# A long convolution by two-stage transforms and a gated token mixer: the first transform group gets a work list of its own

## The chip, the cores and the metric

The kernel runs on one core of a Trainium2 chip. TensorE (PE) multiplies matrices into PSUM; VectorE (DVE) and ScalarE (ACT) empty PSUM and do the elementwise work; GpSimd (POOL) makes index tables and starts some of the transfers, SyncE (SP) most of the others. The metric is the device time of one execution in microseconds (us). Three runs of the kernel before took 2020.13, 2022.82 and 2023.51 us, median 2022.82.

## The reference, cut to what matters

`x` is (8, 5696, 128), `h` is (5696, 128). The first half is a causal convolution along the sequence, per channel, by Fourier transforms; the second mixes its result over the tokens and the channels.

```
Xf, Hf = rfft(x, 2S), rfft(h, 2S)                # S = 5696
x = irfft(Xf * Hf)[:, :S]                        # the convolution
theta = x @ w_theta
y = w_tok_r @ (x*cos(theta)) + w_tok_i @ (x*sin(theta))    # over the 5696 tokens
u = x + y
out = u + relu(u @ w_ch)
```

## The kernel before, in words

**Groups.** The convolution is done in eight groups: two batch entries and half of the channels each (`groups`, dh outer). A group has four stages, each cut into chunks; every chunk fills one of four PSUM buffers (`psum()`, pool of four) and one engine empties it.

- **a** (`stage_a`, L255): 16 chunks of 4 matmuls, a short transform of 89 rows. Its input `x16` has one buffer, loaded by 16 POOL transfers (`load_x`, L139), which can start when the `a` of the group before has read it. The result is emptied by ACT (L262) or by DVE (L260).
- **f** (`spectrum`, L278): 12 chunks of up to 32 matmuls, the second transform, emptied by ACT into a buffer `xs` (L394) of the pool `fs`, which has three.
- **p, q** (`products`, L398): on DVE, per chunk of f one product for each of the two batch entries, of `xs` with the spectrum of `h`, into `uv[0]` and `uv[1]`. The last one of a chunk frees its `xs`.
- **c** (`stage_c`, L419): 16 chunks of 16 matmuls, the way back, emptied by ACT (L425) or DVE (L423) into `g`. Chunks 0 to 7 read `uv[0]`, 8 to 15 read `uv[1]`.
- **d** (`stage_d`, L443): 7 chunks with the twiddle table `e_t` as an operand, emptied by ACT (L449) or DVE (L447) into `yt`, which is stored at the end of the group.

**Work lists.** DVE and ACT run in the order in which the program issues their work (`tc.manual_schedule`). For a group the order is written as a string, `PLAN`, that `run_plan` walks through: a lower-case letter is a chunk emptied by ACT, a capital one emptied by DVE. In the list of group g the letters c and d are group g's, the letters a, f, p and q those of group g+1. `r` is a q that was left over from the group before, for the last chunks (`LATE` of them, three).

**The first group.** It does not go by the list. After `a` of group 0 (`a0`), twelve steps `b_step` (one f, then both its products) run with the two small tables `r_u`, `r_v` woven in (`r_table`, an index part on POOL, then DVE and ACT). Then `woven` merges c of group 0, a of group 1 and the rest of the twiddle tables (`e_left`): `E_STEPS` are seven pieces of five rows, for each of which POOL makes indices (`e_index`, L157, L377, L161), DVE folds them (L164, L167) and ACT takes two sines (L170, L173). The pieces use three areas in the not yet used `yt` buffer and one of their own, `e_more`. After that the letters f, p, q, d, D of `PLAN` run.

**After the groups.** The last group runs with the first 15 phase steps (`phase_step`, in the order of `tile_order`) woven into its c and d. Their input `ya0` is loaded by POOL, its last tile of 128 tokens by SP into a small area (`load_ya0_end`). From about 400 us on the token mixing runs, a long row of matmuls at L1305 that the weights of the ring (L640) feed.

```
PLAN = "aaaAcrAaCaccrArcAacAcAacAcaAcCfCfcpfpCpccqqqfffqpqdfppqffdqpdqpDffpdqfpdpDp"
```

Of the kernel before, what the change touches and what calls it, by code (L numbers as in the profile page):

```python
# [10 lines left out]
F32 = mybir.dt.float32  # L11
BF16 = mybir.dt.bfloat16
# [11 lines left out]
def kernel(  # L24
# [82 lines left out]
    def pool(name, bufs, stack, **kw):  # L107
        return stack.enter_context(tc.tile_pool(name=name, bufs=bufs, **kw))
# [4 lines left out]
    NE, WB, BT = 9, 6 * 4 * CJ * 64, 7 * 1024  # L113
    keep = pool("keep", 1, ctx, side="right")
    fc = pool("fft_c", 1, conv, side="right")
    fs = pool("fft_s", 3, conv, side="right")
    fy = pool("fft_y", 1, conv, side="right")
    s1 = pool("set_1", 1, setup, side="right")

# [43 lines left out]
    def below_one(t, k):  # L163
        nc.vector.scalar_tensor_tensor(t, k, MAGIC, t, op0=ALU.subtract, op1=ALU.subtract)  # L164
# [181 lines left out]
    r_v = fc.tile([P, P], F16)  # L346
    e_t = fc.tile([P, EN, 2, NB], F16)

    def r_table(n_, r_):
        t, k = (s1.tile([P, 2 * N2], F32, name=f"r_{n_}{q}") for q in "tk")  # L350
        index(k, [[0, 2], [1, N2]], 0)
        nc.gpsimd.tensor_scalar(t, k, lane[:, 0:1], 1.0 / N2, op0=mult, op1=mult)
        for q0 in range(2):
            for q1 in range(2):
                a_ = t[64 * q0:64 * q0 + 64, 64 * q1:64 * q1 + 64]
                nc.gpsimd.tensor_scalar(a_, a_, 0.25 * (1 + (1 - n_ if q0 else n_) + q0 - q1), None, op0=add)
        up(t, k, nc.gpsimd)
        below_one(t, k)
        sine(k, t, 1)
        r2, k2 = (z.rearrange("p (r n) -> p r n", r=2) for z in (r_, k))  # L360
        nc.scalar.activation(r2[:, :, :EN], k2[:, :, :EN], AF.Copy, scale=0.125)
        nc.scalar.activation(r2[:, :, EN:], k2[:, :, EN:], AF.Copy, scale=-0.125)

    ES = 5
    e_all = fy.tile([P, NB, N2], BF16, tag="yt", name="e_all").rearrange("p m n -> p (m n)").bitcast(F32)
    first = ExitStack()
    e_more = pool("set_e", 1, first).tile([P, 2 * ES * NB], F32, name="e_more")
    E_STEPS = [(n, n0, min(ES, EN - n0)) for n, n0 in enumerate(range(0, EN, ES))]

    def e_pair(n, cn):  # L370
        at = e_more if n % 4 == 3 else e_all[:, 2 * (n % 4) * ES * NB:]
        return [at[:N1, q * ES * NB:][:, :cn * NB] for q in range(2)]

    def e_index(n, n0, cn):
# [95 lines left out]
    a_chunk, (spectrum, products) = front(0)  # L470
    a0 = steps_of(a_chunk, NA, (2, 4, 6, 8, 10, 12, 14))

    def b_step(c):
        spectrum(c)
        for e in range(2):
            products(c, e)

    b0 = [lambda c=c: b_step(c) for c in range(NCK)]
    BATCH = ((0, 4), (4, 4), (8, 3), (11, 1))
    for c in range(NCK):  # L480
        h_chunk(c)
# [4 lines left out]
        h_store(c0, n)  # L486
    for e_ in E_STEPS[:4]:
        e_index(*e_)
    for t, dst, mul in ((w_in[0], w_theta_sb, 1.0 / (2.0 * math.pi)), (w_in[1], w_ch_sb, 1.0)):
        nc.gpsimd.tensor_scalar(dst, t, mul, None, op0=mult)  # L490
    for n, f in enumerate(a0):
# [138 lines left out]
    def yt_room():  # L630
        return small(0, 4 * P).rearrange("p (b n) -> p b n", b=4)
# [17 lines left out]
    def open_phases():  # L649
# [6 lines left out]
        nc.gpsimd.tensor_scalar(w_neg, w_theta_sb, -1.0, None, op0=mult)  # L656
        st["turns"] = (ones, plus, minus, w_neg)

    def load_ya0():
        sides["phases"]["ya0"] = only = ExitStack()  # L660
        ya = sides["phases"][0] = pool("s2a", 1, only, reuse_waits="tile").tile([P, 4, H - P], BF16, name="ya0")
        for p_ in range(4):
            to = min((p_ + 1) * QR, H - P)
            nc.gpsimd.dma_start(ya[:, :, p_ * QR:to], yt_hbm[:, 0:4, p_ * QR:to])

    def load_ya0_end():
        ya = sides["phases"]["end"] = yt_room()
        nc.sync.dma_start(ya, yt_hbm[:, 0:4, H - P:H])

    def load_ya1(yt=None):  # L670

# [54 lines left out]
    def phase_step(ti, hh, store=nc.sync, odd_eng=None):  # L726

        st = sides["phases"]
        yT = st["end"] if (hh, ti) == (0, 2 * NJ - 1) else st[hh][:, :, ti * P:(ti + 1) * P]
# [24 lines left out]
    steps0 = [lambda ti=ti, n=n: phase_step(ti, 0, nc.gpsimd if 12 <= n < 15 else nc.sync)  # L754
              for n, ti in enumerate(tile_order)]

# [5 lines left out]
                pump()  # L762
        return both

    PLAN = "aaaAcrAaCaccrArcAacAcAacAcaAcCfCfcpfpCpccqqqfffqpqdfppqffdqpdqpDffpdqfpdpDp"
    LATE = PLAN.count("r")
    assert [sum(PLAN.count(x) for x in z) for z in ("aA", "cC", "f", "p", "qr", "dD")] == [NA, NC, NCK, NCK, NCK, ND]

    def ready_for_phases():
        xin.close()  # L770
# [1 line left out]
        load_ya0()  # L772

    def run_plan(plan, g, a_chunk, c_chunk, d_chunk, spectrum, products, late_products):
        at = {"a": 0, "c": 0, "d": 0, "f": 0, "p": 0, "q": 0, "r": NCK - LATE}
# [18 lines left out]
    late_products = None  # L794
# [573 lines left out]
```

## Time and profile before

| | us |
|---|---|
| three runs, median | 2022.82 (2020.13 to 2023.51) |
| the profiled execution | 2024.96 |
| its span | 2023.2 |
| first matmul of f, group 0 | 44.58 |
| first matmul of c, group 0 | 65.40 |
| first matmul of f, group 1 | 88.2 |
| first ACT eviction of a, group 2 | 109.23 |
| first matmul of f, groups 2 to 7 | 125.8, 159.8, 195.9, 233.1, 266.9, 300.8 |
| last d of the last group | 365.0 |

All times are from the start of the span. A row of a timeline gives the start, the time taken, engine, line, operation, output and inputs, and in square brackets how long the engine had been idle and for whom it waited. A row of the windows view gives for a stretch of time its length, the busy time of each engine with its instructions in brackets, then the granted TensorE clock (1.00 is full speed), the share of the DMA engines and GB/s.

### The profile page before, as it was taken

How to read it: one execution, taken by the hardware profiler on the slowest of the kernel's cores; microseconds unless marked ns; L12 is line 12 of the kernel's file. 1: busy time of each engine (PE TensorE's matmuls, PEld its weight loads, DVE VectorE, ACT ScalarE, POOL GpSimd, SP SyncE). 2: the span in 40 equal slices, each digit the busy share in tenths (PEclk: the TensorE clock that was granted, in tenths of full speed). 3: DMA queues.
4: the chain of work that ended last, by engine and by line, in shares of the span. 5: the costliest groups of instructions: out<-in, count | busy, mean ns of one | idle time of the engine just before them, and what ended most of it. 6: DMA issues, size and time to landing. Idle time of an engine off the chain costs nothing.

```text
span 2023.2 us, 41078 instructions
## 1 busy us (share of the span) xinstructions
PE 1929.2 (95%) x15581; PEld 1073.0 (53%) x15757; DVE 1565.0 (77%) x2900; ACT 646.2 (32%) x954; POOL 963.8 (48%) x1721
## 2 busy tenths in 40 slices
PE   5799998889999999999999999999999999999998
PEld 5799897544444444444444444444444444444444
DVE  8877778776788888888877668777677776877767
ACT  6788998742232323232300000011111111111111
POOL 8523323363454545354656554544535445354550
PEclk9789999899999999999999999999999999999999
DMA  9979878997898989899999799887878878788793
GB/s 113 68 85 136 78 103 206 270 257 143 142 184 171 180 170 167 174 174 180 169 172 154 131 243 230 134 149 128 152 130 148 147 129 150 132 150 143 137 156 84
DMA packets 488230, 312.02 MB, mean 154 GB/s; under 512 B 183415, under 2 KB 449143, under 8 KB 487047
## 3 DMA queue, kind: packets, MB, share of 16 engines
q0 software_dynamic: 321552, 155.16, 61.1%
q1 hardware_dynamic: 159312, 140.47, 23.7%
q10 hardware_dynamic: 7168, 13.76, 1.9%
q8 instruction: 123, 2.02, 0.4%
q14 instruction: 75, 0.61, 0.1%
HBM read 354.37 MB, written 90.29 MB: 220 GB/s over the span
## 4 chain that ended last, share of the span: by engine, by line
PE 64%; DVE 4%; DMA 2%; issue 2%; POOL 1%; ACT 0%; DVEq 0%; SPq 0%; POOLq 0%
PE m L1305 59%; DVE c L1312 2%; PE v L985 1%; PE utp L978 1%; POOL ring L640 1%; PE m L1309 1%; DVE wt L898 1%; PE m L1193 1%; DMA b<-z_hbm 1%; DMA ring<-in_moe_w_tok_r_dram 0%; PE theta_ps L524 0%; PE tpz L926 0%; DMA yT<-yt_hbm 0%; DMA c<-cp_hbm 0%; DMA cp_hbm<-c 0%
## 5 line engine op out<-in xcount | busy, mean ns | idle before, releaser
L640 POOL DMA_DIRECT2D ring<-in_moe_w_tok_i_dram x720 | 388.4, 548 | 661.5 <-DVE wt L898 556.5
L898 DVE STREAM_TRANSPOSE wt<-ring 128x384 f32<-128x384 f32 (+2 forms) x720 | 359.0, 522 | 117.2 <-PE m L1305 63.6
L640 POOL DMA_DIRECT2D ring<-in_moe_w_tok_r_dram x720 | 387.2, 549 | 118.7 <-DVE wt L898 66.4
L1305 PE MATMUL m<-b,wt 128*128 128x512 bf16 x1605 | 384.8, 379 | 4.1 <-DVE wt L898 2.1
L1305 PEld LDWEIGHTS <-wt 128*128 128x128 bf16 x1804 | 176.0, 98 | 216.3 <-DVE wt L898 5.1
L1312 DVE TENSOR_TENSOR c<-c,m 128x512 f32<-128x512 f32 x412 | 265.1, 668 | 0.4 <-PE m L1305 0.4
L980 ACT ACTIVATE ring<-utp 128x512 bf16<-128x512 bf16 x85 | 50.8, 597 | 576.3 <-PE utp L978 576.3
L139 POOL DMA_DIRECT2D x<-in_x_dram x128 | 99.4, 792 | 133.7 <-PE ps L255 126.3
L419 PE MATMUL ps<-r_u,uv 128*128 128x128 f16 x1024 | 126.8, 221 | 4.1 <-DVE g__1336 L423 1.2
L419 PE MATMUL ps<-r_v,uv 128*128 128x128 f16 x1024 | 126.3, 221 | 0.0
L1226 PE MATMUL m<-b,wt 128*128 128x512 bf16 x471 | 113.0, 387 | 12.7 <-DMA b<-zr_hbm 7.8
L398 DVE TENSOR_TENSOR uv<-xs,hs 128x1024 f16<-128x1024 f16 (+1 forms) x192 | 116.7, 661 | 10.4 <-ACT xs L394 9.3
L419 PEld LDWEIGHTS <-uv 128*128 128x128 f16 x2048 | 121.3, 99 | 6.0 <-issue 3.9
L975 ACT ACTIVATE ub<-c 128x512 bf16<-128x512 f32 x88 | 55.1, 628 | 185.9 <-DMA ring<-in_moe_w_tok_i_dram 104.0
L394 ACT ACTIVATE xs<-ps 128x1024 f16<-128x1024 f32 x96 | 88.7, 978 | 13.8 <-PE ps L278 8.8
L1226 PEld LDWEIGHTS <-wt 128*128 128x128 bf16 x528 | 51.4, 99 | 70.2 <-issue 16.3
L928 ACT ACTIVATE ring<-tpz 128x512 bf16<-128x512 bf16 (+1 forms) x46 | 27.5, 597 | 146.3 <-PE tpz L926 126.8
L526 ACT ACTIVATE red<-theta_ps,magic 128x512 f32<-128x512 f32 (+1 forms) x46 | 31.6, 687 | 129.4 <-PE theta_ps L524 98.2
L278 PEld LDWEIGHTS <-w_t 64*128 64x128 f16 x3240 | 60.6, 102 | 21.9 <-issue 15.9
L255 PE MATMUL ps<-f_t,x 89*128 89x180 f16 x512 | 56.0, 251 | 7.7 <-DMA x<-in_x_dram 4.8
L987 DVE SCALAR_TENSOR_TENSOR c<-v,c 128x512 f32<-128x512 f32 x88 | 59.8, 682 | 2.6 <-PE v L985 2.6
L831 DVE TENSOR_TENSOR b<-b 128x1024 bf16<-128x1024 bf16 x100 | 61.3, 679 | 0.0
(2928 smaller groups left out, 3632.0 us busy)
## 6 DMA issues: line engine op xcount, KB each, us to landing
ring<-in_moe_w_tok_r_dram POOLq DMA_DIRECT2D x352, 96.0 KB, 4.7
ring<-in_moe_w_tok_i_dram POOLq DMA_DIRECT2D x352, 96.0 KB, 4.9
ring<-in_moe_w_tok_r_dram POOLq DMA_DIRECT2D x352, 80.0 KB, 4.6
ring<-in_moe_w_tok_i_dram POOLq DMA_DIRECT2D x352, 80.0 KB, 3.9
cp_hbm<-c SPq DMA_DIRECT2D x88, 256.0 KB, 2.3
c<-cp_hbm SPq DMA_DIRECT2D x88, 256.0 KB, 4.6
out_dram<-c SPq DMA_DIRECT2D x88, 256.0 KB, 4.6
yy<-y_hbm SPq DMA_DIRECT2D x84, 128.0 KB, 2.5
```

What stands on the lines that cost most here:

```text
L139: nc.gpsimd.dma_start(x16[p0:p1, e, n0:n0 + 16, :HD], bass.AP(tensor=src.tensor, offset=src.offset + (p0 * N2 + n0) * D + dh * HD, ap=[[N2 ...
L278: nc.tensor.matmul(ps[:, e, j * HD:(j + 1) * HD], w_t2[rows, slot(e, c0 + j), N2 * (1 - ri):N2 * (3 - ri)], a_st["a"][rows, ri * K1 + c0 + ...
L394: nc.scalar.activation(xs[:, :, :, :CHK[c][1]], ps, AF.Copy)
L398: nc.vector.tensor_tensor(uv[e][:, :, :, c0:c0 + ck], xs_of[c][:, e:e + 1, :, :ck].to_broadcast([P, 2, HD, ck]), h_part(c), op=mult)
L419: nc.tensor.matmul(o, uv_t[e][:, r, d * K1:d * K1 + P], r_, start=(r == 0), stop=(r == 1))
L640: nc.gpsimd.dma_start(wb[32 * i:32 * i + 32, :ng, :nj * 64], bass.AP(tensor=a.tensor, offset=a.offset + row0 * S + p * H + i * QR + j0 * 6 ...
L831: return [lambda f=f, x=x: f(*x) for f, x in ((nc.vector.tensor_sub, (bt[M3], b12, b22)), (nc.vector.tensor_sub, (bt[M4], b21, b11)), (nc. ...
L898: nc.vector.transpose(wt.rearrange("p j t r -> p (j t r)").bitcast(F32).rearrange("p (j g t) -> p g j t", j=TJ, g=4)[:, :ng, :nj], wb[:, : ...
L987: nc.vector.scalar_tensor_tensor(c[:m], v[:m], 0.0, c[:m], op0=ALU.max, op1=ALU.add)
L1226: nc.tensor.matmul(ms[n // 2 * 2 + h], a[n][:, j, :, r], bts_of[p][jj][n % 2 * 2 + h][:, r, :], start=(n % 2 == 0 and jj == 0 and r == 0), ...
L1305: nc.tensor.matmul(ms[q], a[q][:, j, :, r], bts[jj][q][:, r, :], start=(jj == 0 and r == 0), stop=(jj == NJ - 1 and r == 1 and q not in left))
L1312: nc.vector.tensor_tensor(c, z, ms[q], op=op)
```

## The change

- The first group goes by lists. `PLAN_X` holds f, p, q of group 0 and `u`, the two small tables; it leaves four q over. `PLAN_0` is the list of group 0 with c, d of group 0, a, f, p, q of group 1, those four q as `r`, and `t`, a piece of the twiddle table: its `e_table` and then the `e_index` of the piece four further on.
- `fs` has four buffers instead of three, and four products are late instead of three.
- `PLAN`, the list of the later groups, is another: of 16 a, 10 are emptied by ACT instead of 8; of 7 d, 4 instead of 5; the first four f, instead of three, stand before the last c.
- The index part of both small tables (`r_index`) is issued with the first indices of the twiddles, and their first DVE step (`below_one`) stands in front of the list. In the built program POOL makes the four first index sets, then those of the small tables one after the other; DVE has the two folding steps behind the tenth and the twelfth of the twelve evictions at L333, so before its first eviction of `a0`.
- The twiddle pieces have four rows (`ES`): nine pieces in four areas of the `yt` buffer; `e_more` goes.
- For room, `ya0` holds 19 tiles instead of 21. Tiles 19 and 20 are loaded by SP into an `xs` buffer when the late products of the last group are issued (`load_ya0_ends`), and their phase steps are the 13th and 14th.

```diff
-    fs = pool("fft_s", 3, conv, side="right")
+    fs = pool("fft_s", 4, conv, side="right")
...
-    def r_table(n_, r_):
-        t, k = (s1.tile([P, 2 * N2], F32, name=f"r_{n_}{q}") for q in "tk")
+    r_at = {}
+
+    def r_index(n_):
+        t, k = r_at[n_] = [s1.tile([P, 2 * N2], F32, name=f"r_{n_}{q}") for q in "tk"]
...
         up(t, k, nc.gpsimd)
-        below_one(t, k)
+
+    def r_table(n_, r_):
+        t, k = r_at[n_]
         sine(k, t, 1)
...
-    ES = 5
+    ES = 4
...
-        at = e_more if n % 4 == 3 else e_all[:, 2 * (n % 4) * ES * NB:]
+        at = e_all[:, 2 * (n % 4) * ES * NB:]
...
     for e_ in E_STEPS[:4]:
         e_index(*e_)
+    for n in range(2):
+        r_index(n)
...
-    woven(b0, ([lambda: r_table(0, r_u), lambda: r_table(1, r_v)], 0.0, 0.6))
-    e_left = [lambda f=f, n=n: f(*E_STEPS[n]) for f, n in (
-        (e_table, 1), (e_index, 5), (e_table, 2), (e_index, 6), (e_table, 3),
-        (e_table, 4), (e_table, 5), (e_table, 6))]
+    for n in range(2):
+        below_one(*r_at[n])
+    PLAN_X = "fqfpqpfffupfqppfqfqpqppqfqffpfuppp"
+    PLAN_0 = "cttCCrcaCaAraraarAaAaacaattAACcftCCpffcfttpCPccccctpqfqfqpfqfpDqddfqpqqfpdpfDpddfppp"
+    PLAN = "aaAarcAarcAaCaacrAarcAacAacCfpfcCccffpCppcccqfqfqfqqpDfqddppfpqdpqfDpffdpDp"
+    LATE = PLAN.count("r")
+    at_ = {"f": 0, "p": 0, "q": 0, "u": 0}
+    for k in PLAN_X:
+        n, at_[k] = at_[k], at_[k] + 1
+        if k == "f":
+            spectrum(n)
+        elif k == "u":
+            r_table(n, (r_u, r_v)[n])
+        else:
+            products(n, "pq".index(k))
...
+    Y_ENDS = 19
...
+    def load_ya0_ends():
+        two = fs.tile([P, 2, HD, CK], F16, tag="xs", name="ya_end").rearrange("p e d k -> p (e d k)").bitcast(BF16)
+        ends_ = sides["phases"]["end"]
+        for q, ti in enumerate(range(Y_ENDS, 2 * NJ - 1)):
+            ends_[ti] = two[:, 4 * P * q:4 * P * (q + 1)].rearrange("p (b n) -> p b n", b=4)
+            nc.sync.dma_start(ends_[ti], yt_hbm[:, 0:4, ti * P:(ti + 1) * P])
...
+    tile_order[12:] = [19, 20] + [ti for ti in tile_order[12:] if ti not in (19, 20)]
...
+            elif k == "t":
+                e_table(*E_STEPS[n])
+                if n + 4 < len(E_STEPS):
+                    e_index(*E_STEPS[n + 4])
...
             for c in range(NCK - LATE, NCK):
                 late_products(c, 1)
+            load_ya0_ends()
...
-        plan = PLAN
-        if g == 0:
-            woven((steps_of(c_chunk, NC, [n for n in range(NC) if n % 2 or n < 8]), 0.06, 1.0),
-                  (steps_of(a_chunk, NA, (5, 11)) + [lambda: load_x(2)], 0.0, 0.55), (e_left, 0.0, 0.9))
-            first.close()
-            plan = [x for x in PLAN if x in "fpqdD"]
-        run_plan(plan, g, a_chunk, c_chunk, d_chunk, spectrum, products, late_products)
+        run_plan(PLAN if g else PLAN_0, g, a_chunk, c_chunk, d_chunk, spectrum, products, late_products)
```

More of the change, by code (lines that the diff above doesn't have):

```diff
@@ L471 @@
     a0 = steps_of(a_chunk, NA, (2, 4, 6, 8, 10, 12, 14))
[L473 to L478, printed above, removed]
     BATCH = ((0, 4), (4, 4), (8, 3), (11, 1))
@@ L498 @@
     in_order.enter_context(tc.manual_schedule(engines={mybir.EngineType.DVE, mybir.EngineType.Activation}))
-    woven(b0, ([lambda: r_table(0, r_u), lambda: r_table(1, r_v)], 0.0, 0.6))
-    e_left = [lambda f=f, n=n: f(*E_STEPS[n]) for f, n in (
-        (e_table, 1), (e_index, 5), (e_table, 2), (e_index, 6), (e_table, 3),
-        (e_table, 4), (e_table, 5), (e_table, 6))]
+    for n in range(2):
+        below_one(*r_at[n])
+    PLAN_X = "fqfpqpfffupfqppfqfqpqppqfqffpfuppp"
+    PLAN_0 = "cttCCrcaCaAraraaarAaAaacaattAACcftCCpffcfttpCCccctpqfqfqpfqfpDqddfqpqqfpdpfDpddfppp"
+    PLAN = "aaAarcAarcAaCaacrAarcAacAacCfpfcCccffpCppcccqfqfqfqqpDfqddppfpqdpqfDpffdpDp"
[9 more added lines that the diff above has]
+            products(n, "pq".index(k))
+    assert at_ == {"f": NCK, "p": NCK, "q": NCK - PLAN_0.count("r"), "u": 2}
     setup.close()
@@ L657, in open_phases @@
         st["turns"] = (ones, plus, minus, w_neg)
+    Y_ENDS = 19
     def load_ya0():
         sides["phases"]["ya0"] = only = ExitStack()
-        ya = sides["phases"][0] = pool("s2a", 1, only, reuse_waits="tile").tile([P, 4, H - P], BF16, name="ya0")
+        ya = sides["phases"][0] = pool("s2a", 1, only, reuse_waits="tile").tile([P, 4, Y_ENDS * P], BF16, name="ya0")
         for p_ in range(4):
-            to = min((p_ + 1) * QR, H - P)
+            to = min((p_ + 1) * QR, Y_ENDS * P)
             nc.gpsimd.dma_start(ya[:, :, p_ * QR:to], yt_hbm[:, 0:4, p_ * QR:to])
     def load_ya0_end():
-        ya = sides["phases"]["end"] = yt_room()
+        ya = yt_room()
+        sides["phases"]["end"] = {2 * NJ - 1: ya}
         nc.sync.dma_start(ya, yt_hbm[:, 0:4, H - P:H])
+    def load_ya0_ends():
[4 more added lines that the diff above has]
+            nc.sync.dma_start(ends_[ti], yt_hbm[:, 0:4, ti * P:(ti + 1) * P])
     def load_ya1(yt=None):
@@ L728, in phase_step @@
         st = sides["phases"]
-        yT = st["end"] if (hh, ti) == (0, 2 * NJ - 1) else st[hh][:, :, ti * P:(ti + 1) * P]
+        yT = st["end"][ti] if hh == 0 and ti in st["end"] else st[hh][:, :, ti * P:(ti + 1) * P]
         if hh:
@@ L763, in with_load @@
         return both
-    PLAN = "aaaAcrAaCaccrArcAacAcAacAcaAcCfCfcpfpCpccqqqfffqpqdfppqffdqpdqpDffpdqfpdpDp"
-    LATE = PLAN.count("r")
-    assert [sum(PLAN.count(x) for x in z) for z in ("aA", "cC", "f", "p", "qr", "dD")] == [NA, NC, NCK, NCK, NCK, ND]
+    for plan, late in ((PLAN_0, PLAN_0.count("r") - LATE), (PLAN, 0)):
+        assert [sum(plan.count(x) for x in z) for z in ("aA", "cC", "f", "p", "qr", "dD")] == [
+            NA, NC, NCK, NCK, NCK + late, ND]
+    assert PLAN_0.count("t") == len(E_STEPS) - 1
     def ready_for_phases():
@@ L774, in run_plan @@
     def run_plan(plan, g, a_chunk, c_chunk, d_chunk, spectrum, products, late_products):
-        at = {"a": 0, "c": 0, "d": 0, "f": 0, "p": 0, "q": 0, "r": NCK - LATE}
+        at = {"a": 0, "c": 0, "d": 0, "f": 0, "p": 0, "q": 0, "t": 1, "r": NCK - plan.count("r")}
         for x in plan:
@@ L793 @@
     late_order, pool_order = ExitStack(), ExitStack()
-    late_products = None
+    late_products = products
     for g, (bp, dh) in enumerate(groups):
```

2 lines of the change are left out of this document (removed).

## The prediction

> **What bounds the kernel now.** I read the page first, for the engines over the whole span, then the windows view for the first 126 us and for one later group, then the waits of the later groups, and last the timelines of the front. TensorE fills 95% of the span:
>
> ```profile
> PE 1929.2 (95%) x15581; PEld 1073.0 (53%) x15757; DVE 1565.0 (77%) x2900; ACT 646.2 (32%) x954; POOL 963.8 (48%) x1721
> ```
>
> The token mixing after 400 us is not touched by the change, so only the convolution can move the time; what it saves arrives at the end whole, since everything behind it is started by its results. The windows view of the front (length, busy us of PE, PEld, DVE, ACT, POOL, granted clock, DMA):
>
> ```profile
> 44.20:52.00 7.80, 5.41 (x240) 5.27 (x242) 3.87 (x7) 5.19 (x9) 7.53 (x10) 0.78 1.21 204
> 52.00:63.60 11.60, 3.91 (x132) 3.46 (x124) 9.79 (x18) 7.43 (x11) 8.03 (x8) 0.50 1.80 136
> 63.60:69.00 5.40, 5.39 (x43) 5.40 (x44) 3.54 (x6) 4.24 (x7) 4.58 (x5) 0.50 0.01 3
> 69.00:88.20 19.20, 17.21 (x280) 16.72 (x278) 17.48 (x22) 14.37 (x22) 10.04 (x14) 1.00 0.49 32
> 88.20:96.40 8.20, 5.61 (x267) 4.94 (x267) 6.51 (x11) 6.76 (x9) 4.85 (x7) 1.00 1.76 111
> 96.40:108.40 12.00, 11.91 (x234) 11.23 (x227) 8.41 (x14) 9.20 (x12) 0.00 (x0) 0.50 0.01 3
> 108.40:113.40 5.00, 5.00 (x42) 5.00 (x40) 2.40 (x5) 3.30 (x5) 0.00 (x0) 0.50 0.72 146
> 251.70:285.40 33.70, 32.34 (x813) 30.98 (x811) 27.67 (x38) 31.36 (x37) 12.01 (x16) 1.00 0.90 90
> ```
>
> From 44 to 63.6 us (f, p, q of group 0) PE idles half the time; behind each thin stretch the clock stands at 0.50, at 52 to 69 and again at 96.4 to 113.4, where PE at half speed has no idle time left (11.91 of 12.00). A later group (last row) takes 33.7 us with PE busy for 32.3. There PE hardly ever waits for an engine:
>
> ```profile
> PE ps L278 <- issue: 5.8, 7, 1.5
> PE ps L443 <- issue: 5.1, 3, 2.0
> PE ps L255 <- ACT yt L449: 0.9, 3, 0.3
> PE ps L278 <- ACT xs L394: 0.5, 2, 0.3
> ```
>
> (108.5 to 320 us: who waited for whom, us, times, longest.) The 10.9 us of "issue" are no wait for a result, and a new order does not take them away. What the front waits for (ACT, DVE, then PE):
>
> ```profile
> 49.05 0.40 ACT L170 ACTIVATE r_0k<-r_0t,zero_b 128x128 f32<-128x128 f32 x1 [1.85 <-DVE r_0t L164]
> 54.76 0.40 ACT L170 ACTIVATE r_1k<-r_1t,zero_b 128x128 f32<-128x128 f32 x1 [2.14 <-DVE r_1t L164]
> 46.32 2.50 DVE L398 TENSOR_TENSOR uv<-xs,hs 128x1024 f16<-128x1024 f16 x4 [2.16 <-ACT xs L394]
> 56.54 7.92 DVE L398 TENSOR_TENSOR uv<-xs,hs 128x1024 f16<-128x1024 f16 x14 [1.81 <-ACT xs L394]
> 63.61 0.65 PE L255 MATMUL ps<-f_t,x 89*128 89x180 f16 x3 [4.83 <-DMA x<-in_x_dram]
> ```
>
> ACT and DVE wait for each other around each small table, DVE needs until 64.4 for 24 products, and PE could not start `a` of group 1 earlier anyway, because its input lands at 63.6.
>
> **The change part by part.** *Index of the small tables on POOL, before `a0`.* POOL's rows:
>
> ```profile
> 27.74 1.98 POOL L356 TENSOR_SCALAR r_0t<-r_0t 64x64 f32<-64x64 f32 x2
> 37.99 0.70 POOL L356 TENSOR_SCALAR r_1t<-r_1t 64x64 f32<-64x64 f32 x2
> 42.82 0.54 POOL L161 TENSOR_SCALAR r_1k<-r_1t 128x128 f32<-128x128 f32 x1
> 44.02 7.71 POOL L139 DMA_DIRECT2D x<-in_x_dram  x10 [0.67 <-PE ps L255]
> ```
>
> An index set of 445 columns takes 0.54 + 0.74 + 1.36 = 2.64 us, start to start (23.51 to 25.64, end 27.00); one of 267 took 1.95 (76.03 to 77.98); between them, 2.30 for 356. Four from 23.51 on end at 32.7. A small table takes 0.39 + 0.46 + 0.67 + 0.88 + 0.57 = 2.97, so the second is ready at 38.6. DVE is ready for its fold at 37.3 (the last L333 ended at 37.04, and the other fold takes 0.28). It waits 1.3 us and then folds 0.28, and its evictions of `a0`, which it empties without a gap from 37.41 to 44.1, start about 1.5 late; a smaller twiddle piece gives back 0.1. Queued behind it: f of group 0, and the load of group 1's input, whose first transfer waits for PE's last `a0` (44.02). Both shift by 1.4, and the input lands at 65.0 instead of 63.6. Bounds: 0 (POOL's 43.4 for its whole list holds gaps that vanish) to 2.7 (both pairs at 0.99 apiece, as at 27.74). [...]
>
> *`PLAN_X`.* Removed from before c: 4 products. With the folds done early, four buffers, and the tables only after the fifth and the last f, ACT needs 11 × 0.95 + 0.40 + 2 × 0.74 = 12.3 us and DVE 19 × 0.62 (2.50 for 4) + 0.39 = 12.2, both without the two stops; an `xs` is free by the time it is wanted (chunk 4's eviction is due 3.7 us after chunk 0's, whose two products end 2.3 after it starts). The first product starts at 46.3 + 1.4 = 47.7, the last ends at 59.9, and c starts there instead of at 65.40.
>
> *`PLAN_0`.* Four chunks of c come ahead of the first a. At half clock a chunk takes 16 × 0.107 = 1.71 us (65.40, 65.51, ...), at full clock 16 × 0.0556 = 0.89: they end between 63.5 and 66.7, just where the input lands (65.0). So its wait is filled. I put ACT at the first a at 67.0. ACT is the fullest engine of the list: 11 a × 0.70, 8 c × 0.96, f 10.9, d 4 × 0.89 + 0.45, tables 7 × 0.98 + 0.5 (two sines of 445 columns every 1.12, of 267 every 0.82) = 37.6; PE has 14.2 + 6.4 + 5.9 + 5.8 = 32.3 at full clock; DVE about 36. Of ACT's, 3.9 (two c, two tables) lie before the first a. 67.0 + 33.7 = 100.7, and 1.4 of stops as in the later group (33.7 - 32.3): 102.1, where ACT before reached the first a of group 2 at 109.23. Gain 7.1. Bounds: 2 (PE sinks to half clock in f and d as at 96.4, where 12.0 us of PE time would be about 7 at full speed) to 9 (no stops, and the 2.0 that the stage from 108.5 to 125.8 takes over the 15.3 of its like come back).
>
> *The list of the later groups.* Moved to ACT: two a (1.40), to DVE one d (0.89 on ACT). ACT goes from 31.4 to 31.9 busy in 33.7, DVE falls a little, PE keeps its 32.3. What bounds the group stays: 0 for six groups. Bounds: -1 in all (the 1.4 us of waits of PE) to +0.9 each, if the 0.5 does not fit between ACT's evictions and stops it as long again.
>
> *The end.* One more late product lies before the last group's c: 0.62; DVE there waited 1.22 for PE (323.28 to 324.50), which covers it, so 0 to 0.6, I take 0.6. Two loads join SP's queue at about 324, where one of the same size took 2.50: 5 us, in front of the first store of `y` and the `zz` stores. Seven `zz` and six `y` buffers, with a step every 2.7 us, hide a delay of 5. Without that cover it would be up to 3.
>
> Sum against the profiled execution (2024.96, span 2023.2): -7.1 + 0 + 0.6 = -6.5, span 2016.7. It lies 2.1 above the median of the runs, so the difference is put on the median: 2022.82 - 6.5 = 2016.3.
>
> **The rivals.** *No change that counts (0.24).* The front gains 7.1, but PE sinks to half clock in f and d, which leaves 2 to 4, or each later group loses 0.5. For it: the 0.50 rows come after stretches with PE at 5.61 of 8.20, and `PLAN_0` with ACT in front leaves PE at 32 of 38. Against: in the later groups, PE at 17 of 18.5 in f and d, the clock mostly stays. Time 2020.5.
>
> *The clock stays up (0.13).* Neither 96.4 to 113.4 nor the start of group 2's a and c is at 0.50: 2 us more, and no stops: 2013. [...] Here the longest gap of PE from 88.2 to 96.4 was 1.35, and the clock fell; the measurement decides, so a thin stretch is enough. [...]
>
> *Slower (0.09).* The list of the later groups makes ACT the bound: in each a-and-c part ACT has two a more, and PSUM's four buffers fill. Its place is the stretch up to the last c, where ACT gets 21.3 us of work beside PE's 22; with the 1.5 to 2 us of short waits that ACT has there now it comes to 23, so 0.7 to 1 a group, and a PE that waits falls to 0.50 for a window (171.5 to 174.9 shows one of 3.4 us), 1.7 more. From 1.1 a group the front's gain is gone; at 2.4 in six groups it is 14.4 - 6.5 = +8: 2031. Against it: today's waits of PE for ACT are 1.4 us in all.
>
> **How the numbers follow.** The forecast has 0.54, its own range 2013 to 2019. The range over the cases: down to 2009.5 (9 in the front, 1.4 if DVE does not wait for POOL, 1 in the later groups, and 1.7, half of what the three runs differ by), and up to 2023.5, the first rival's 2020.5 with 3 of SP's delay; outside lie most of the slow rival and little of the rest. No change means within 0.2%, 4 us, about what this measurement can tell from no change: faster is below 2018.8. The forecast gives 0.50 of its 0.54 to it, the clock 0.13, which makes 0.63; same 0.28 (0.24 and 0.04 of the forecast); slower 0.09.
>
> **What would show it.** In the changed profile: DVE waiting about 1.3 us for POOL in front of the second fold (none: the first term is too large; over 2.7: too small); the first c at 59.9 (58 to 61.5), and no wait of PE for `x` over 1 us; the first a of group 2 emptied at 102 (100 to 107); the later groups at 33.7 us each; the last d 6 us earlier than 365.0. The prediction is wrong if ACT or DVE stops PE in the later groups, if the piece of twiddles that POOL indexes behind group 2's loads comes late and DVE waits in its order, or if the half-clock stretches move to where PE is full.

## The result, and the profile after

| | us, median (lowest to highest) | ratio to the kernel before (95% interval) |
|---|---|---|
| before, beside it | 2023.16 (2020.13 to 2025.93, 4 runs) | |
| changed | 2009.99 (2009.51 to 2012.36, 4 runs) | 0.9929 (0.9909 to 0.9949) |

The changed kernel is faster by 0.7%: the medians lie 13.2 us apart, and the ratio makes it some 14, where 6.5 were forecast. The median of 2009.99 lies below the forecast's own range (2013 to 2019) and at the low end of the range over all cases (2009.5 to 2023.5). The profiled execution took 2009.51, its span 2007.7, which is 15.5 under the span before. Where that comes from can be read off the time at which the last matmul of `d` of each group starts:

| last d of group | 0 | 1 | 2 | 3 | 4 | 5 | 6 | 7 |
|---|---|---|---|---|---|---|---|---|
| before | 108.3 | 144.2 | 180.3 | 217.8 | 251.6 | 285.2 | 320.6 | 365.0 |
| after | 100.6 | 134.4 | 168.2 | 205.2 | 238.2 | 270.7 | 303.9 | 350.6 |

The front gained 7.7, the lists of the six later groups 9.0 (16.7 at group 6), and the last group gave 2.3 back: 14.4 at 350.6. Behind it 1.1 more came. The windows view of the changed kernel by these stages (length, busy us and instructions of PE, PEld, DVE, ACT, POOL, granted clock, DMA share, GB/s):

```profile
47.60:62.20 14.60, 7.36 (x360) 6.98 (x360) 11.96 (x22) 12.47 (x19) 12.72 (x17) 0.85 1.68 131
62.20:68.60 6.40, 6.39 (x64) 6.39 (x65) 3.77 (x6) 2.95 (x5) 2.08 (x3) 0.53 0.07 6
68.60:100.60 32.00, 29.51 (x740) 27.68 (x737) 30.53 (x47) 31.71 (x45) 22.42 (x28) 1.00 0.76 48
168.20:205.20 37.00, 32.28 (x813) 30.89 (x809) 26.62 (x37) 31.94 (x40) 11.96 (x16) 1.00 1.06 130
238.20:270.70 32.50, 31.89 (x812) 30.76 (x809) 26.56 (x37) 31.76 (x40) 11.95 (x16) 1.00 0.94 93
303.90:350.60 46.70, 39.92 (x589) 35.21 (x595) 35.18 (x60) 35.76 (x56) 17.44 (x36) 0.93 1.00 245
```

Four chunks of c run at half clock (62.2 to 68.6, PE without idle time); then the clock stands at 1.00 until 303.9. The half-clock stretch of before at 96.4 to 113.4 has no successor. `PLAN_0` from the first a of group 1 to its last d takes 32.00, and ACT is busy for 31.71 of it. A later list without trouble takes 32.5 (238.2 to 270.7, the list of group 5); the list of group 3 (168.2 to 205.2) takes 37.0 at full clock with PE busy for 32.3, so it has 4.7 us of waits.

All six later groups in one row, before and then after:

```profile
108.40:320.60 212.20, 199.79 (x4851) 191.43 (x4849) 166.26 (x228) 190.18 (x222) 63.90 (x85) 0.96 0.85 106
```

```profile
100.60:303.90 203.30, 192.89 (x4860) 185.14 (x4858) 162.07 (x224) 191.67 (x231) 64.00 (x85) 1.00 0.89 110
```

PE's waits in the second stretch (who waited for whom: us, times, longest; the last three lines, which make 1.4 us, are left out):

```profile
PE ps L421 <- issue: 4.1, 2, 2.1
PE ps L445 <- issue: 2.0, 2, 1.0
PE ps L278 <- issue: 1.5, 1, 1.5
PE ps L445 <- ACT xs L396: 1.2, 3, 0.4
...
```

So 212.2 is 199.8 busy, 10.9 of "issue" and some 1.4 of other waits; 203.3 is 192.9, 7.6 and 2.6. Of the 8.9 that went, 6.9 are busy time of PE at the same number of matmuls, with the clock at 1.00 instead of 0.96, and 3.3 are "issue" waits; other waits grew by 1.2.

Not all of this is the work of the later groups' list. The first 5.0 us of the stretch before (108.4 to 113.4) run at the half clock that began at 96.4 in the front, and PE is busy all the time there; that is some 2.5 us (an estimate: half of 5.0) which the changed front saves and not the list. List by list, from the table, the six gains are 2.1, 2.3, 0.5, 0.8, 1.1 and 2.2. In the fourth and the fifth the clock stands at 1.00 in both kernels, so what is gained there owes nothing to the clock.

The front in the timeline of the changed kernel (start, time taken, engine, line, operation; in brackets the idle time before it and what ended it):

```profile
37.09 0.29 DVE L164 SCALAR_TENSOR_TENSOR r_0t<-r_0k,r_0t 128x128 f32<-128x128 f32 x1 [1.14 <-POOL r_0k L161]
40.02 0.29 DVE L164 SCALAR_TENSOR_TENSOR r_1t<-r_1k,r_1t 128x128 f32<-128x128 f32 x1 [1.83 <-POOL r_1k L161]
...
50.32 11.83 DVE L400 TENSOR_TENSOR uv<-xs,hs 128x1024 f16<-128x1024 f16 x20 [2.64 <-ACT xs L396]
```

```profile
48.19 5.38 PE L278 MATMUL ps<-a__753,w_t 64*128 64x64 f16 x245 [0.86 <-ACT a__753 L262]
55.36 1.83 PE L278 MATMUL ps<-a__753,w_t 64*128 64x64 f16 x107 [1.79 <-issue]
...
62.21 0.29 PE L421 MATMUL ps<-r_u,uv 128*128 128x128 f16 x1 [4.46 <-DVE uv L400]
```

DVE waits for POOL at both small tables, 2.97 us in all; its twenty products follow without a stop, and c starts at 62.21.

### The profile page after: what moved, and what is told of

It is laid out like the page before. It is cut to its first block, busy times and chain, and to the rows that moved or that the text cites. A ratio compares the mean times of both kernels' runs of the same rounds, so it can differ in the third digit from the quotient of the medians.

```text
span 2007.7 us, 41091 instructions
## 1 busy us (share of the span) xinstructions
PE 1920.4 (96%) x15581; PEld 1064.4 (53%) x15757; DVE 1557.9 (78%) x2897; ACT 646.5 (32%) x965; POOL 963.0 (48%) x1727
## 4 chain that ended last, share of the span: by engine, by line
PE 66%; DVE 4%; DMA 3%; issue 2%; ACT 0%; POOL 0%; DVEq 0%
PE m L1326 61%; DVE c L1333 2%; DMA b<-z_hbm 1%; PE utp L999 1%; PE v L1006 1%; PE m L1330 1%; DVE wt L919 1%; PE m L1214 1%; PE theta_ps L534 0%; PE tpz L947 0%; DMA c<-cp_hbm 0%; DMA cp_hbm<-c 0%; DMA z_hbm<-mag 0%; DVE b L852 0%; PE m L1247 0%
## 5 line engine op out<-in xcount | busy, mean ns | idle before, releaser
L400 DVE TENSOR_TENSOR uv<-xs,hs 128x1024 f16<-128x1024 f16 x192 | 117.7, 661 | 7.5 <-ACT xs L396 5.9
L278 PEld LDWEIGHTS <-w_t 64*128 64x128 f16 x3240 | 54.2, 97 | 12.1 <-issue 5.9
L556 ACT ACTIVATE mag<-red 128x512 f32<-128x512 f32 (+1 forms) x46 | 29.0, 631 | 92.9 <-DVE red L538 92.9
```

The costliest lines, as they stand in the source:

```text
L400: nc.vector.tensor_tensor(uv[e][:, :, :, c0:c0 + ck], xs_of[c][:, e:e + 1, :, :ck].to_broadcast([P, 2, HD, ck]), h_part(c), op=mult)
```

## The experiments

Two readings competed at first: the gain beyond the forecast comes from the later groups' list ("list"), or the front or the fourth spectrum buffer carries it. The changed kernel and the front with the old list:

**e0_changed**: no edit.

> The changed kernel again, beside its variants on one chip. Every theory: about 14 us under the kernel before (ratio 0.993), of it 8 by the end of the last d of group 0 and 9 in the six groups behind it, no half clock between 70 and 300 us.

Measured: 0.9923 (0.9900 to 0.9946); 2008.67 us. The clock did fall once between 70 and 300 us in this trace, at 191.6, where nothing of the kind was expected.

**e1_old_list**: the front of the changed kernel, the later groups by the list of before.

```
-    PLAN_0 = "...pdpfDpddfppp"
-    PLAN = "aaAarcAarcAaCaacrAarcAacAacCfpfcCccffpCppcccqfqfqfqqpDfqddppfpqdpqfDpffdpDp"
+    PLAN_0 = "...pdpfDpddfppqp"
+    PLAN = "aaaAcrAaCaccrArcAacAcAacAcaAcCfCfcpfpCpccqqqfffqpqdfppqffdqpdqpDffpdqfpdpDp"
```

> New front and four buffers, the old list for the later groups (three late products; the first list does one product more, to fit). Theory 'list': the 9 us of the later groups came from their new list, so here only the front is gained, 7 to 8 us (ratio 0.9962), the groups take 33.7 to 36 us each and the clock falls to half in some f and d stretches as before. Theory 'front': a front that ends at full clock carries the rest, so 12 us or more stay (ratio under 0.9942), groups under 34, no half clock between 70 and 300 us. Theory 'buffer': the fourth buffer alone does it, then also 12 or more.

Measured: 0.9959 (0.9943 to 0.9974). So the front alone is worth 0.41%, 8.3 us, with an interval of 5.3 to 11.5; the prediction's sum for it was 6.5. The rest goes with the list.

**e2_old_front** and **e3_old_both**: the kernel before with the four buffers, the smaller pieces of the twiddle table, and the changed end, but its own order of the first group; e2 with the changed list, e3 with the old one.

```
-    fs = pool("fft_s", 3, conv, side="right")
+    fs = pool("fft_s", 4, conv, side="right")
-    ES = 5
+    ES = 4
...
+            load_ya0_ends()
...
-    PLAN = "aaaAcrAaCaccrArcAacAcAacAcaAcCfCfcpfpCpccqqqfffqpqdfppqffdqpdqpDffpdqfpdpDp"
+    PLAN = "aaAarcAarcAaCaacrAarcAacAacCfpfcCccffpCppcccqfqfqfqqpDfqddppfpqdpqfDpffdpDp"
```

(The last pair of lines is in e2 only.)

> Old order of the first group (with twiddle pieces of four rows), four buffers, the new list for the later groups. Theory 'list': 6 to 9 us under before (ratio 0.9955 to 0.997), the groups at 32.5 to 33.8 us except the one with the reload of h, no half clock from 115 to 300 us though it is there at 52 to 69 and 96 to 113. Theory 'front': at most 2 us, half-clock windows behind 115 us as before. Theory 'buffer': 6 to 9 as well.

> Old order of the first group and old list, but four buffers, twiddle pieces of four rows and the two end tiles loaded apart. Theories 'list' and 'front': within 2 us of before, groups at 33.7 to 36 us, half-clock windows as before. Theory 'buffer': 6 to 9 us under before, with the groups as short as in the changed kernel.

Measured: e2 0.9981 (0.9963 to 1.0000), e3 1.0026 (1.0007 to 1.0045). The list is worth 0.45% with the old front and 0.36% with the new one (0.9959 to 0.9923), 7 to 9 us both times, with some 4 us either way (an estimate from the spread of the runs); the trace of the changed kernel shows 9.0 less the 2.5 of the front's clock, so some 6.5. The buffers, the pieces and the end without the new order cost some 5 us, so the fourth buffer is no gain by itself, and the order of the first group, measured from e3, is worth 0.67%. Because of these 5 us both came out slower than expected: e3 was to be within 2 us of before, and e2 6 to 9 us under it, which is also more than the 4 us that it gained. What of e3 costs them was not taken apart.

**e4_r_first**: the changed kernel with the small tables' indices ahead of the twiddles' on POOL, against the 2.97 us of DVE's waits.

```
-    for e_ in E_STEPS[:4]:
-        e_index(*e_)
     for n in range(2):
         r_index(n)
+    for e_ in E_STEPS[:4]:
+        e_index(*e_)
```

> The changed kernel with POOL's indices of the two small tables in front of the four index sets of the twiddles. Theory 'fold': the 1.14 and 1.83 us that DVE waits for POOL before a of group 0 are on the path, with the half clock that follows them; they go, the last a of group 0 ends near 44 us instead of 47.6, and the time falls by 2 to 4 us against the changed kernel (ratio to before 0.991 to 0.992). Rival: the input of group 1 or the warm-up of TensorE hides it, then within 1 us of the changed kernel.

Measured: 0.9922 (0.9892 to 0.9951), no different from the changed kernel. DVE and PE in its front:

```profile
48.70 7.92 DVE L400 TENSOR_TENSOR uv<-xs,hs 128x1024 f16<-128x1024 f16 x13 [2.64 <-ACT xs L396]
58.04 4.00 DVE L400 TENSOR_TENSOR uv<-xs,hs 128x1024 f16<-128x1024 f16 x7 [1.41 <-ACT xs L396]
```

```profile
46.57 5.41 PE L278 MATMUL ps<-a__753,w_t 64*128 64x64 f16 x245 [0.86 <-ACT a__753 L262]
56.61 2.86 PE L278 MATMUL ps<-a__753,w_t 64*128 64x64 f16 x115 [4.63 <-issue]
62.10 0.29 PE L421 MATMUL ps<-r_u,uv 128*128 128x128 f16 x1 [2.62 <-DVE uv L400]
```

Both folds now run without a wait, and f and the products begin 1.6 earlier (46.57 for 48.19, 48.70 for 50.32). But PE then stands for 4.63 us on "issue" after the same 245 matmuls, DVE gets a gap of 1.41, and c starts at 62.10 instead of 62.21. In the changed kernel itself DVE sets the start of c: its products begin late, at 50.32, and run for 11.83 without a stop, in spite of the 1.79 that PE waits in f. With the wait for POOL gone, PE's wait in f takes its place, so nothing is gained by the removal. Of a warm-up of TensorE the traces show this much: in the changed kernel c begins at 62.21 at half clock, and the clock stands at 1.00 from 68.2 on.

**e5_r_first_tail**: as e4, and the group before the last by a list whose last product is not behind the last two d.

```
+    PLAN_L = PLAN.removesuffix("ffdpDp") + "ffpdpD"
-        run_plan(PLAN if g else PLAN_0, g, ...
+        run_plan((PLAN_L if g + 2 == len(groups) else PLAN) if g else PLAN_0, g, ...
```

> The same, and in the list of the last but one group the last product of the first batch entry comes before the last d that DVE empties. Theory 'tail': the 1.97 us that TensorE waits for that product at the start of the last group fall to about 1.4, and the time by 0.5 us. Rival: the next wait takes its place, no change beside e4.

Measured: 0.9913 (0.9891 to 0.9936), not separable from e4 by time. The first c of the last group in the changed kernel, and in e5:

```profile
306.71 0.23 PE L421 MATMUL ps<-r_u,uv 128*128 128x128 f16 x1 [1.97 <-DVE uv L400]
```

```profile
304.92 0.22 PE L421 MATMUL ps<-r_u,uv 128*128 128x128 f16 x1 [1.36 <-DVE yt L449]
```

The last group takes 44.2 in e5 (302.7 to 346.9), 46.7 in the changed kernel, where a half-clock window lies behind the wait (307.1 to 310.6), and 47.1 in e4 with the same wait of 1.97 and a window too. In the trace the edit gives the end's 2.3 back, as the wait fell from 1.97 to 1.36 and no half-clock window follows; the timed runs do not resolve it.

**e6_f_twice**: the kernel before with every matmul of f of group 1 done twice, to fill the thin stretch at 88 to 96, behind which the clock had fallen.

```
-            for ri in range(2):
+            for ri in [0, 1] * times:        # times = 2 in group 1
```

> The kernel before with every matmul of f of group 1 done twice (the same sums, started anew), which gives TensorE 5.9 us of work more in the stretch from 88 to 108 us, where it was busy for 5.6 of 8.2 us before the clock fell at 96.4. Theory 'thin stretch': the clock falls because TensorE is too little busy there, so it now stays at 1.00 through 96 to 113, d of group 0 takes about 0.9 instead of 1.56 us a chunk, and in spite of 5.9 us of extra work the first f of group 2 comes no later than 2 us after 125.8 (perhaps sooner). Rival: the clock falls by itself or by load, then 96 to 113 stays at 0.50 and the extra work is added, 4 to 8 us on the time.

Measured: 1.0046 (1.0028 to 1.0064). Between 94.9 and 113 the half clock falls from 17 us to 6.8, so with the stretch filled the clock stayed up for most of it; but the matmuls took more than that gave, and the last d of group 0 ends at 115.4 instead of 108.3. In the later groups, whose lists are those of before, the "issue" waits grew from 10.9 to 15.4: they moved here when the instructions ahead of them changed.

**What of the list does it.** The changed list differs up to the last c (the a come earlier, ten c instead of seven stand behind the last a and between the f, ten a on ACT instead of eight) and behind it (f further apart, three d on DVE). e7, e8, e9, e11 and e12 are the changed kernel with another list, e10 is the changed kernel again. The old order in e7 has a fourth `r` and a fourth f with its p ahead of the changed part, so that the letters come out even.

**e7_old_head**, **e8_old_tail**, **e9_f_spread**, **e10_changed_again**:

```
 changed  PLAN = "aaAarcAarcAaCaacrAarcAacAacCfpfcCccffpCppccc" "qfqfqfqqpDfqddppfpqdpqfDpffdpDp"
 e7       PLAN = "aaaAcrAaCaccrArcAacrAcAacAcaAcCfCfcpfpCpccfp" "qfqfqfqqpDfqddppfpqdpqfDpffdpDp"
 e8       PLAN = "aaAarcAarcAaCaacrAarcAacAacCfpfcCccffpCppccc" "qqqffqdfppqffdqpdqpDffpdqfpdpDp"
 e9       PLAN = "aaAarcAarcAaCaacrAarcAacAacCfpfcCccffpCppccc" "qfqDfpqdfpqdfpqDfpqdfpqdfpqfpDp"
```

> The changed kernel; the later groups' list has the old one's order up to the last c (8 a on each of ACT and DVE) and the changed one's order of f, p, q and d behind it. Theory 'tail' (the old list's runs of f use up PE's instructions faster than they are fetched, PE waits for 'issue' and its clock falls behind the wait; the changed tail has the f further apart): as the changed kernel, 0.992 of the kernel before (0.990 to 0.994), the 'issue' waits of PE from the last d of group 0 to that of group 6 in all 6 to 8 us. Rival 'head' (the gain comes from the two a more that ACT empties and from the order of a and c): as the changed kernel with the whole old list, 0.996, 'issue' 9 to 13 us. Rival 'phase' (where the waits fall is a matter of the length of the instruction stream alone): 0.994, and no tie of the waits to the list.

> The changed kernel; the later groups' list has the changed order up to the last c and the old one's order of f, p, q and d behind it (f in runs of two and three, five d on ACT). Theory 'tail': the list's gain goes, 0.996 of the kernel before (0.994 to 0.998), 'issue' waits 9 to 13 us in the same stretch, and half-clock windows of 3.4 us that begin within 2 us of such a wait. Rival 'head': as the changed kernel, 0.992, 'issue' 6 to 8 us. Rival 'phase': 0.994.

> The changed kernel; in the later groups' list no two f stand next to each other behind the last c but the last pair: f and d take turns, with one p and one q for each. Theory 'tail', carried on: fewer 'issue' waits than the changed kernel's 7.6 us (3 to 6), no half-clock window in the later groups, 0.990 to 0.992 of the kernel before. Rival 'products': with one f at a time DVE's products set the pace, PE waits for ACT and DVE instead, 0.993 to 0.997.

> The changed kernel unchanged, beside the three others on the same chip: 0.992 of the kernel before (0.990 to 0.994), 'issue' waits 6 to 8 us in the same stretch. Every half-clock window between the last d of group 0 and that of group 6 begins within 2 us of the end of an 'issue' wait of PE of over 0.9 us; a window without such a wait would speak against the tie.

Measured: e7 1.0067 (1.0039 to 1.0096), e8 0.9924 (0.9900 to 0.9949), e9 0.9956 (0.9938 to 0.9973), e10 0.9935 (0.9911 to 0.9958). My theory "tail" falls: with the old order behind the last c (e8) the gain stays, and with the changed order there but the old one ahead (e7) it turns into a loss of 0.7%. "Head" takes its place as to where the gain lies, but its own marks were missed too: e7 was to come out at 0.996 with 9 to 13 us of "issue" waits and came out at 1.0067 with 2.1, and e8 has 4.6 us of them where 6 to 8 were expected. In e10, the changed kernel itself, they come to 8.9, also outside 6 to 8. The windows of the six later groups of e7, the largest group of PE's waits there, and the windows of e8:

```profile
100.20:327.50 227.30, 214.76 (x4859) 205.86 (x4860) 172.64 (x236) 189.63 (x219) 64.17 (x85) 0.89 0.78 99
```

```profile
PE ps L278 <- ACT xs L396: 6.8, 6, 1.5
```

```profile
98.90:303.90 205.00, 196.92 (x4857) 189.66 (x4857) 157.79 (x219) 195.64 (x237) 64.10 (x85) 0.98 0.86 108
```

In e7 PE hardly waits on "issue" (2.1 us), but 1.4 to 1.5 us for an `xs` in four of the groups, and the clock falls to 0.89: PE's busy time is 22 us above the changed kernel's (214.8 for 192.9) with only 2 us more of waits (12.2 for 10.2). In e9 the "issue" waits fall to 3.8, as foreseen, while the others rise to 7.6, and 13.6 us at half clock come behind one of 1.33: its rival "products" was right.

**e11_new_a8** and **e12_old_a10**: the changed order with eight a on ACT, the old order with ten.

```
 e11      PLAN = "aaAarcAarcAaCaAcrAArcAacAacC..."     (the rest as changed)
 e12      PLAN = "aaaAcraaCaccrArcaacAcAacAcaAc..."    (the rest as old; PLAN_0 as in e1)
```

> The changed kernel, its later groups' list in the changed order, but with eight a on ACT and eight on DVE as in the old list (it has ten and six). Theory 'order' (the a come earlier, ten c instead of seven stand behind the last a and between the f, and PE has c to do while ACT and DVE empty f): as the changed kernel, 0.992 to 0.9935 of the kernel before, few PE waits of over 0.9 us in the stretch from the last d of group 0 to that of group 6 (at most 3). Rival 'engines' (DVE, with two a fewer, is in time with its products): as with the old list, 0.995 to 0.998.

> The changed kernel with the old list's order for the later groups, but ten a on ACT and six on DVE as in the changed list. Theory 'order': as with the old list, 0.995 to 0.998 of the kernel before, five or more PE waits of over 0.9 us in the same stretch. Rival 'engines': as the changed kernel, 0.992 to 0.9935.

Measured: e11 0.9953 (0.9937 to 0.9969), e12 0.9983 (0.9970 to 0.9996). A group without long waits at full clock, of e11, of e12 and of the changed kernel run again (e10):

```profile
238.90:272.20 33.30, 32.38 (x809) 30.83 (x808) 28.05 (x40) 30.82 (x37) 12.01 (x16) 1.00 0.92 91
```

```profile
99.50:134.50 35.00, 32.94 (x816) 31.22 (x817) 27.77 (x40) 33.05 (x42) 11.99 (x16) 1.00 0.87 87
```

```profile
238.70:271.20 32.50, 31.79 (x808) 30.50 (x807) 26.66 (x38) 31.66 (x39) 11.98 (x16) 1.00 0.94 93
```

Neither part has the gain by itself. The ten a on ACT gain nothing in the old order (35.0 and 34.5 for the two undisturbed groups of e12, against 33.6 to 33.8 with the old list), so "engines" alone falls. But "order" alone does not hold either: the order with eight a took 33.3 here and 0.9953 in all, which lies in the range of "engines" (0.995 to 0.998) and has four long waits where "order" allowed three. Its interval overlaps that of the changed kernel (0.9911 to 0.9958 in e10), and by how much the two a count within the changed order stays open. All the stretches side by side, by the profiled executions (last d of group 0 to that of group 6, us; waits of PE of 0.9 us or more in it):

| | list: head, a on ACT, tail | stretch | long waits | clock |
|---|---|---|---|---|
| before, e1, e3 | old, 8, old | 212.2, 214.6, 211.3 | 6, 6, 5 | 0.96, 0.97, 0.97 |
| e6 (f of group 1 twice) | old, 8, old | 217.9 | 8 | 0.95 |
| e12 | old, 10, old | 214.8 | 5 | 0.98 |
| e7 | old, 8, changed | 227.3 | 5 | 0.89 |
| e11 | changed, 8, changed | 207.0 | 4 | 1.00 |
| e9 | changed, 10, spread | 213.5 | 3 | 0.97 |
| e8 | changed, 10, old | 205.0 | 2 | 0.98 |
| changed, e0, e10, e2 | changed, 10, changed | 203.3, 204.9, 205.8, 203.0 | 5, 2, 2, 1 | 1.00, 0.99, 0.99, 0.99 |
| e4, e5 | the same (e5 but for one group) | 210.2, 202.9 | 3, 5 | 0.95, 1.00 |

**Lists without a long wait.** Long waits are not the whole of it. In lists with no wait of 0.9 us or more and the clock at 1.00 throughout, the old list takes 33.6 to 33.8 us, 33.7 in the mean (four of them, in the traces of before, e1 and e3), the changed one 32.5 to 33.8, 33.0 in the mean (twelve, in the three profiles of the changed kernel). That is some 0.7 a group and about 4 us in six (an estimate), without any help of the clock.

**Waits and the clock.** In the stretches of all fifteen traces there are 24 stays at half clock that begin there. Every one of them begins within 3 us of the end of a wait of PE of 0.92 us or more; in e8, e9 and e10, as their expectations had it, within 2 us of one on "issue". The waits behind which the clock fell in the kernel before, and the windows of two of these stays:

```profile
171.09 1.57 PE L278 MATMUL ps<-a__3277,w_t 64*128 64x64 f16 x62 [1.52 <-issue]
...
211.41 2.10 PE L443 MATMUL ps<-e_t,g__4297 89*128 89x89 f16 x36 [1.43 <-issue]
...
311.27 0.54 PE L443 MATMUL ps<-e_t,g__7210 89*128 89x89 f16 x6 [1.67 <-issue]
```

```profile
171.40:174.90 3.50, 3.50 (x85) 3.41 (x78) 3.14 (x6) 3.02 (x4) 0.00 (x0) 0.51 1.95 188
212.40:215.80 3.40, 3.40 (x89) 3.17 (x86) 2.25 (x4) 2.02 (x3) 0.00 (x0) 0.50 0.02 5
```

In e7 the same happens behind a wait for ACT, and in e4, whose list is the changed one, behind one for "issue" (the row of PE's timeline and the window behind it, e7 first):

```profile
127.15 0.64 PE L278 MATMUL ps<-a__2317,w_t 64*128 64x64 f16 x32 [1.40 <-ACT xs L396]
```

```profile
127.20:139.30 12.10, 11.83 (x247) 11.12 (x247) 9.46 (x15) 9.35 (x11) 0.00 (x0) 0.58 0.32 23
```

```profile
128.06 1.71 PE L445 MATMUL ps<-e_t,g__2343 89*128 89x89 f16 x28 [1.69 <-issue]
```

```profile
128.80:135.60 6.80, 6.80 (x147) 6.23 (x145) 3.60 (x6) 4.59 (x5) 0.00 (x0) 0.50 0.02 5
```

Not every such wait was followed by a stay: there are 62 waits for the 24. The changed list does not make the clock safe either (e4: 0.95); it has fewer of these waits, 1 to 5 where the old one has 5 to 8.

What sorts the waits, for the most part, is where they fall in time. In each trace the changes of the granted clock lie on a grid of 3.41 us (before, in the stretch: 113.42, 171.45, 174.86, 212.41, 215.82, 311.40, 314.81), and the waits sort by the share of one such window in which PE was busy. Of the 875 windows at full clock in the stretches, PE was busy for 0.25 to 0.63 in the 24 behind which the clock fell; of the other 851 only 11 are as low as that. In the changed kernel and in e10 the same wait of 2.14 us stands at the same place. In e10 it lies within one window, and the clock falls at the end of it; in the changed kernel it is cut in two by the end of a window, and the clock stays (e10 first):

```profile
188.80:192.20 3.40, 1.26 (x24) 1.24 (x23) 0.82 (x1) 1.10 (x2) 1.84 (x4) 1.00 1.82 125
192.20:195.60 3.40, 3.40 (x39) 3.20 (x38) 1.65 (x4) 2.09 (x3) 1.82 (x3) 0.51 1.54 95
```

```profile
187.70:191.10 3.40, 1.97 (x79) 1.72 (x77) 0.23 (x1) 3.06 (x4) 2.00 (x3) 1.00 2.23 159
191.10:194.50 3.40, 2.69 (x49) 2.69 (x49) 2.27 (x3) 1.38 (x2) 2.87 (x4) 1.00 1.93 116
```

## Why the prediction was wrong in size

**Direction and front: right, in part by luck.** The front's term was 7.1, up to the first a of group 2 on ACT, which was emptied at 101.91 for 109.23 before and 102.1 in the forecast: 7.3. e1 gives 8.3 (5.3 to 11.5), with the forecast's own assumption that the list counts for nothing. But two misses of nearly the same size cancel here. (The list of the built kernel is `PLAN_0 = "cttCCrcaCaAraraaarAaAaacaattAACcftCCpffcfttpCCccctpqfqfqpfqfpDqddfqpqqfpdpfDpddfppp"`; it has the 11 a and 8 c on ACT of the forecast's sum.)

The first miss lies ahead of c. The wait for POOL was put at 1.3 (0 to 2.7) and is 2.97, past its bound. The two small tables took POOL 2.93 and 2.96, as put; the four index sets took 10.45 (23.61 to 34.06) instead of 9.2, and the second and the third of them, 2.78 and 2.99, were the long ones. That the small tables' pairs of 64x64 would be the short ones (0.70 before, at 37.99, and not 1.98, at 27.74) was the author's estimate; two pairs took 1.55 in each table (34.88 and 37.81). Nor was the wait for POOL all: with it removed (e4), f still begins at 46.57 for 44.58 before. The clock stands at 0.50 from 37.5 to 51.1 in the changed kernel, through most of `a0` and the start of f, where it was 1.00 until 45.2 before, and the sum had no term for that. So the first product began at 50.32 instead of 47.7, and as the products took 11.83, near the 12.2 of the sum, c started at 62.21 instead of 59.9. The input loads begin 3.6 later than before (47.64 for 44.02), not 1.4. No wait for `x` followed, as forecast: four c at half clock lie ahead of the first a, up to 68.6.

The second miss is `PLAN_0`, which made up for it. ACT was to go from the first a at 67.0 to 102.1, 35.1 us with 1.4 of stops; it went from 69.75 to 101.91, 32.2, and was busy all the time. Its work had been put at 33.7, 1.5 too much, and the stops did not come. That the clock stays up here, a rival with a chance of 0.13, was right from 68.6 to 307.1, and with it came the start of group 2 at full clock, which the forecast had left out of its sum and which is worth some 2.5 (the rival had put it at 2).

**The list of the later groups: the step that failed.** "What bounds the group stays: 0 for six groups", with a bound of -1 in all. In the trace it was -9.0, of which some 6.5 are the list's, and the pairs e3/e2 and e1/e0 give 7 to 9. The argument counted the busy time of each engine in one clean group and found PE at 32.3 both times. It had two errors. "The 10.9 us of 'issue' are no wait for a result, and a new order does not take them away": they fell to 7.6, went to 15.4 in e6 where nothing in these lists was changed, and to 2.1 in e7. And PE's 199.8 busy us were taken for its work; part of them was the same work at half clock, behind the long waits and, in the first 5 us, behind the front. In the changed kernel the same matmuls took 192.9. The group lengths of before would have told: two lists of before took 33.6 and 33.8 at a clock of 1.00, four took 35.4 to 37.5 at 0.93 to 0.95. The bound of -1 failed with it: it rested on the 1.4 us that PE waits for other engines in six groups, while the lists without a long wait alone became shorter by some 4. The runs place the gain ahead of the last c (e7, e8); which letters there give it stays open.

**The end: right in kind, short in size.** 0.6 was put down for the late product in front of the last group's c, on the ground that DVE's wait for PE covers it. PE waited 1.97 there instead of 0.97, for the last p of the list; the clock fell for 3.4 us behind it, and the last group took 2.3 longer (46.7 for 44.4). In e5, which takes that p ahead of the last d, it takes 44.2. Whether the added late product lengthens this wait is not shown. SP's loads were hidden, as forecast: the mixing begins 14.5 earlier than before, and the last d ended 14.4 earlier.

## What to carry to other kernels

Where PE is nearly full, look at its busy time together with the granted clock: in these traces 24 waits of 0.92 to 2.83 us were followed by 3.4 us or more at half clock, in which the same matmuls took nearly twice as long (in the changed kernel one of c every 0.107 us behind 62.2, every 0.056 at full clock), so a list that avoids such a wait can be worth more than its length: 3.4 us at half clock cost 1.7, and the longest stay here, 17.1, cost 8.5 (estimates, with PE busy throughout). Do not take an "issue" wait for a constant of the program (in the six later groups 10.9 us before, 15.4 in e6, 2.1 in e7), and do not credit a wait that is removed until the next thing that the engine waits for has been named: e4 took 1.6 us out of DVE's way and PE waited it away.

## What the runs showed of the hardware

**The long "issue" waits of PE end behind packets of the instruction queue.** The queue table of the changed kernel's page, and its first line of busy times:

```profile
PE 1920.4 (96%) x15581; PEld 1064.4 (53%) x15757; DVE 1557.9 (78%) x2897; ACT 646.5 (32%) x965; POOL 963.0 (48%) x1727
```

```profile
q8 instruction: 123, 2.02, 0.4%
```

PE's 15581 matmuls and 15757 weight loads are 31338 instructions, 255 for each of the 123 packets, all of 16,384 bytes. e6, with 720 PE instructions more, has 126 packets. In the trace's packet records of this queue one starts shortly ahead of each long "issue" wait's end: of the 62 long waits of the fifteen stretches 58 are on "issue", and all 58 end 2.2 to 3.5 us after a packet began, though the packets came only about every 5 us there (in the changed kernel 39 begin from 100.79 to 302.53). In the front of the changed kernel it started at 53.13 and took 0.94, and PE went on at 55.36, 1.3 later; in e4 at 54.09 and 0.93, and PE went on at 56.61, 1.6 later. f took instructions fastest (in the changed kernel 32 matmuls, with as many weight loads, in the 0.57 us from 265.26, where d had 20 in the next 0.95), and 47 of the 58 stand in f and d. No run changed the fetching itself, so that PE waits for these packets is an inference; when a packet is asked for, the trace does not show, and in e4 it came a microsecond later although PE had stopped 1.6 earlier (at 51.98 for 53.57).

**The clock fell behind waits shorter than one window of 3.41 us.** In the stretches the long wait of PE at the start of each of the 24 stays was one of 0.92 to 2.83 us, and a stay lasted 3.4 us or a multiple, up to 17.1 in e7. The longest wait of all, 3.15 in e0, had no stay behind it (it was cut by the end of a window at 181.4, with PE busy for 0.55 and 0.53 of the two). A window with PE busy for 0.25 to 0.63 of it stood ahead of every stay, and 11 windows as low as that had none behind them. The grid does not lie at the same place in every trace: one of its edges is at 191.1 in the changed kernel, at 191.6 in e0 and at 192.2 in e10. Of these three profiles of the very same kernel, two have one stay, at 191.6 and 192.2, and one has none, behind waits at the same places of the list of group 3. What ends a stay the traces do not show: PE was busy for 0.86 to 1.00 of every window at half clock in the stretches, of those behind which the clock rose and of those behind which it did not.
